# Attention, Fourier mixing and MLP on one core: another PSUM bank for one bound, and landmark sums tied to the planner's clock

## The chip, the core and the metric

The kernel runs on one core of a Trainium2 chip. The time of a run is device microseconds. TensorE (PE) multiplies matrices; VectorE (DVE), ScalarE (ACT) and GpSimd (POOL) work on elements; SyncE (SP) starts the DMAs. Each engine runs its own queue in order, and what one engine writes for another is handed over by semaphores. PE writes into eight PSUM banks of 2 KB in each partition.

## What is computed

The input is q, k and v for 8 batches, 8 heads, 576 tokens and 64 columns a head, and two weights. First comes attention over 32 landmarks a head (each is the mean of 18 tokens):

```python
q_lm = q.reshape(B, H, m, S // m, D).mean(axis=3)
k_lm = k.reshape(B, H, m, S // m, D).mean(axis=3)
A = sm(q, k_lm); Bm = sm(q_lm, k_lm); C = sm(q_lm, k)      # softmaxes
Z = Bm.transpose(0, 1, 3, 2) / (norm1(Bm) * norminf(Bm) + 1e-06)
for _ in range(6):
    Z = 2 * Z - Z @ Bm @ Z
x = A @ Z @ C @ v
```

Then `x` (heads side by side: 576 x 512 a batch) gets the real part of its 2-D Fourier transform added, each token is normalised, and an MLP follows:

```python
u = x + real(fft(fft(x, axis=1), axis=2))
un = (u - mu) / np.sqrt(var + 1e-06)
return u + np.maximum(un @ w_ch1, 0.0) @ w_ch2      # 512 -> 2048 -> 512
```

## The kernel before

Batches are counted from 0, as `b`. The MLP works on chunks of 256 tokens (`TCH` = 2 tiles of 128), of which the 8 batches give 18. Its factors are split into a high and a low half in float16, and each product is three PE products: hi x hi, hi x lo, lo x hi. `h<-unT,w` is its first product, `acc<-w,h` its second; between them ACT and DVE turn a PSUM bank `h` into the tile `h` (ACT the high half, DVE the low one). `unT` is the normalised, transposed tokens of a chunk, `u` the tokens before normalising; `u<-acc` is DVE's last sum, which frees a bank `acc`.

PSUM is divided by hand: four banks are called `at` and serve all of the attention, two are called `h` (`PSH` = 2), two `acc`. A new `at` or `h` tile takes the bank that was used longest ago, and its first product waits until all readers of that bank are done.

The order of PE's instructions is set by a planner at build time. `Kernel.run` holds threads (Python generators), in order of priority: attention (with its helpers `landmarks` and `values`), weights, MLP. A clock `self.now` advances by an estimated cost for each PE instruction. A thread yields how long it wants to be left alone; `till(...)` gives that from the planned end (`self.there`) of the tiles that it needs and from the planned readers of `at` banks, plus a margin. While attention pauses, the MLP's products are put into the queue. In batches 0 and 1 the weights are still being scaled and split (`w<-w,wsc`), and where there is nothing to do yet, PE multiplies a constant (`idle`) so that it doesn't stand.

DVE, ACT and POOL get their order from a scheduler that has its own model of times. The class `Timed` wraps the three: it estimates when each instruction starts, and can tie an instruction behind another of the same engine. The number `late` does that: the instruction is held behind the last one whose planned start is not after `late`.

```python
late = max([late] + [self.kernel.there.get(key(a), 0.0) for a in aps if key(a) in self.kernel.slow and a is not out])
...
prev = next((p for s, p in reversed(self.log) if s <= late), None)
```

`late` is zero unless the code sets it, or the instruction reads something marked as slow (a load, a DMA transpose, a result of POOL). Without such a tie the scheduler may put an instruction wherever its own model finds room.

What happens in one batch, with the names that the profile shows:

- `tokens` starts with the landmark sums `lm`: six DVE reductions over groups of 18 tokens of the loads `big` (per half `e` of the heads: one of k with 1152 elements, two of q with 576 each), and ACT's sums of |q| (`big,amax`). From them come powers of two as scales: `kmax`, `qsum`, `aq_e`, `aq_r` (its reciprocal), `kb`, and by one small product with a matrix of ones (`at<-kb,ones`) and `power` the scale `ak_e`. This is `bound`. Then q and the landmarks are split into halves (`big<-big,aq_r`: ACT writes the high half, DVE the low one; per half of the heads one of 1024 and one of 128 elements).
- `landmarks` computes the logits of the landmarks of q against those of k, and against all of k (`at<-big,lm`, four `at` banks at once). DVE takes `Bd` out of the first two, makes its softmax (`bmx`, `bs`), `nrm` (the softmax and a diagonal of its sums), and `BT`, `BTd`; it takes maxima of all four (`cmx`, `cb`), and ACT writes their exponentials as `mid`. With the banks free again, PE multiplies `nrm` by ones (`at<-nrm,ones_bd`), and six Newton steps follow (`at<-RE,E`).
- `values` transposes the exponentials. From batch 2 on: ACT and POOL split them, two DMA transposes write them back, DVE adds the two halves (`mid<-mid`, 128 x 640), and PE multiplies by v (`at<-big,mid`).
- `mix` multiplies everything together per 128 tokens: `w<-at,scw` is a Fourier term, `u` the sum. `norm` follows: `bn`, `mv`, `ve`, `rt`, `r`, then `row<-u,mv,r`, which ACT casts and POOL or DVE subtracts, and two DMA transposes a tile (`unT<-row`). In batches 0 and 1 the last steps differ a little; up to chunk 1 PE transposes.

The landmark sums of the next batch need only its loads, so DVE may run them early, during the mix of the batch before.

Of the kernel before, what the change touches and what calls it, by code (L numbers as in the profile page):

```python
# [10 lines left out]
F32 = mybir.dt.float32  # L11
# [7 lines left out]
P = 128  # L19
# [16 lines left out]
MARGIN, NM, AM, M0 = 1.5, 2.0, 2.0, 0.2  # L36
# [11 lines left out]
HOLD = 2.5  # L48
# [110 lines left out]
class Kernel:  # L159
# [82 lines left out]
    def mm(self, out, a, b, start=True, stop=True, share=1.0):  # L242
        self.there[out.name] = self.now
        self.now += share * (1.0e-3 if a.dtype == F32 else 0.42e-3) * math.prod(b.shape[1:])
        self.nc.tensor.matmul(out, a, b, start=start, stop=stop, skip_group_check=True)  # L245

    def tr(self, out, a, ident):
        self.there[out.name] = self.now
        self.now += 0.11
        self.nc.tensor.transpose(out, a, ident)  # L250
# [7 lines left out]
        self.A.activation(hi, src, AF.Copy, scale=scale)  # L258
        self.V.scalar_tensor_tensor(lo, src, scale, hi, ALU.mult, ALU.subtract)

    def bound(self, cols, n, factor, name):

        ps = self.psum()
        self.mm(ps[:, :n], self.ones16, cols[:, :n])
        return self.power(ps[:, :n], n, factor, name)

# [155 lines left out]
    def tokens(self, b, st):  # L422

        nc, mm, mm3, tr, sm, split = self.nc, self.mm, self.mm3, self.tr, self.sm, self.split
        V, A = self.V, self.A
# [5 lines left out]
        qhs = []  # L431
        for e in range(2):
            kf, qf = loads[e][0][:, 0 : 2 * S], loads[e][1][:, 0:NQ]
            first = V.tensor_reduce(lm[:, 1, e], kf.rearrange("p (m t) -> p m t", t=18), AX.X, ALU.add)
            if b == 1:
                self.tc.keep_in_program_order(first)

            lv = lm[:, 0, e].rearrange("p (x o m) -> p x o m", o=2, m=8)
            qv = qf.rearrange("p (x o t) -> p x o t", o=2, t=2 * SEG)
            for o in range(2):  # L440
                first = V.tensor_reduce(lv[:, :, o], qv[:, :, o, o : o + 144].rearrange("p x (m t) -> p x m t", t=18), AX.X, ALU.add)
                if b == 1:
                    self.tc.keep_in_program_order(first)
            qhs.append(self.big().bitcast(F16))
            A.activation((self.whole[0].bitcast(F16) if b == 0 else qhs[e])[:, 0:NQ], qf, AF.Abs, accum_out=am[:, e : e + 1])
            yield self.till(lm)
        kb = self.small(2, "kb", BF16)
# [5 lines left out]
        V.tensor_tensor(qs, am[:, 0:1], am[:, 1:2], ALU.add)  # L453
        eq, rq = self.power(qs, 1, 2.0**-13, "aq", b == 1)
        V.tensor_tensor(kb[:, 0:1], km, eq, ALU.mult)
        yield self.till(kb, banks=1, more=AM) + (HOLD if b == 1 else 0.0)
        ek, rk = self.bound(kb, 1, 2.0**-13, "ak")
        sc = self.small(2, "sc")
        V.tensor_tensor(sc[:, 0:1], eq, rk, ALU.mult)
        V.tensor_scalar(sc[:, 1:2], ek, 1.0 / 144.0, None, ALU.mult)  # L460
# [19 lines left out]
        for u in range(3):  # L480
            yield self.till(*qhs, banks=1)
            ps = self.psum()
# [27 lines left out]
        for u in range(3):  # L510
            ae, w = aes[u], 512 if u < 2 else 128
            AT = (self.mid() if u < 2 else self.row()).bitcast(F16)[:, 0 : 2 * w].rearrange("p (y t) -> p y t", y=2)
            if b < 2:
                yield self.till(ae, banks=1)
                ps = self.psum()
# [3 lines left out]
            if b >= 2 or u == 2:  # L519
                yield self.till(ae)  # L520
                hl = self.row(2 * w, F16).rearrange("p (y t) -> p y t", y=2)
# [43 lines left out]
    def values(self, b, st, loads, Ces, crs, ci):  # L565

        nc, mm, tr, sm = self.nc, self.mm, self.tr, self.sm
        V, A = self.V, self.A
        R0 = sm.tile([P, 2, 64], F32, name="R0", bufs=1)
        ETs = []  # L570
        for g in range(2):
            yield self.till(Ces[g])
            if b < 2:
                ET = self.mid().rearrange("p (t m) -> p t m", t=5)
                ps = self.psum()
                for t in range(4):
                    tr(ps[:, 128 * t : 128 * t + 128], Ces[g][:, 128 * t : 128 * t + 128], self.ident)
                A.copy(ET[:, 0:4].rearrange("p t m -> p (t m)"), ps)
                ps = self.psum()
                tr(ps[:64, 0:128], Ces[g][:, 512:576], self.ident)  # L580
                A.copy(ET[:64, 4], ps[:64, 0:128])
            else:

                hl, th = (self.mid().bitcast(F16).rearrange("p (y t) -> p y t", y=2) for _ in range(2))
                A.copy(hl[:, 0], Ces[g])
                self.G.tensor_tensor(hl[:, 1], Ces[g], hl[:, 0], ALU.subtract)
                for y in range(2):
                    nc.sync.dma_start_transpose(th[:, y].rearrange("p (t m) -> p t m", m=P), hl[:, y])
                self.there[th.name] = self.there[hl.name] + 4.0
                self.slow.add(th.name)  # L590
                V.tensor_tensor(Ces[g], th[:, 0], th[:, 1], ALU.add)
                ET = Ces[g].rearrange("p (t m) -> p t m", t=5)
            ETs.append(ET)
        for g in range(2):
            yield self.till(ETs[g], loads[0][2], loads[1][2], banks=1)
            vfs = [loads[e][2].rearrange("p (c d) -> p c d", c=5) for e in range(2)]
            ps = self.psum()
            for t in range(5):
                n = P if t < 4 else 64
                for i in range(4):  # L600
                    e, at = divmod(sum(GROUPS, []).index(HEADS[g][i]), 4)
                    v = vfs[e][:n, t, 64 * at : 64 * at + 64]
                    mm(ps[32 * i : 32 * i + 32, 0:64], ETs[g][:n, t, 32 * i : 32 * i + 32], v if at % 2 == i % 2 else v[:, ::-1], t == 0, t == 4)
            V.tensor_scalar(R0[:, g], ps[:, 0:64], crs[g], ci[:, g : g + 1], ALU.mult, ALU.mult)
        st["R0"] = R0
# [480 lines left out]
```

## Time and profile before

| | |
|---|---|
| runs (three) | 1008.21, 1006.84, 1006.77 us; median 1006.84 |
| profiled execution | 1008.58 us, of which the span is 1006.8 |
| PE, matmuls | 959.8 us busy, 95% of the span, 8698 instructions |
| DVE | 600.5 us, 60% |
| ACT | 333.0 us, 33% |
| POOL | 102.8 us, 10% |
| DMA | 74.66 MB moved, mean 74 GB/s |
| costliest PE groups | first product 411.4 us, second product 386.2 us |
| all landmark sums on DVE | 48, 44.4 us |

A row of the timeline has the start in us, the busy time, the engine, the code line, the operation, the output and inputs by name with the shape, and a count where equal instructions follow each other; in brackets stands how long the engine stood before it, and what it waited for. All lines are 245 (products) or 138 (DVE, ACT and POOL, through `Timed`), so one goes by the names. A row of the windows has the stretch, its sum and mean length, and then for PE, the weight loads, DVE, ACT and POOL the busy time with the number of instructions, then the granted clock of PE and the DMA share.

### The profile page before, as it was taken

What the parts mean: (1) busy time and instruction counts of PE and PEld (TensorE: products, weight loads), DVE (VectorE), ACT (ScalarE), POOL (GpSimd) and SP (SyncE); (2) the same over time, 40 slices, a digit from 0 to 9 for tenths busy, and PEclk for the clock granted to TensorE, in tenths of its full rate; (3) what the DMA queues carried; (4) which work ended last, traced back from release to release, by engine and by line L of the source; (5) the groups of instructions that cost most, each with busy time, mean ns of one, the idle gap of its engine ahead of it and who ended that gap; (6) DMA issues with size and microseconds to landing.
All of it is one profiled execution on the core that took longest, in us unless ns stands there. A gap on an engine that the chain in (4) does not pass through costs nothing.

```text
span 1006.8 us, 20849 instructions
## 1 busy us (share of the span) xinstructions
PE 959.8 (95%) x8698; PEld 666.9 (66%) x8698; DVE 600.5 (60%) x1629; ACT 333.0 (33%) x716; POOL 102.8 (10%) x114
## 2 busy tenths in 40 slices
PE   6869989699999999999999999999999999999998
PEld 4658556467766767667666677676666776666665
DVE  7989876878476836388367736684643935241111
ACT  5668543243224322143224222332322323111110
POOL 0000000003011301032012201120020210010000
PEclk8879989989999999999999999999999999999999
DMA  9854104123302340134211340225020200120000
GB/s 330 290 210 145 62 2 169 22 54 83 136 17 48 63 157 12 32 51 100 100 43 29 45 168 9 55 44 187 1 53 22 53 10 22 22 54 21 1 21 21
DMA packets 97774, 74.66 MB, mean 74 GB/s; under 512 B 68112, under 2 KB 86544, under 8 KB 97552
## 3 DMA queue, kind: packets, MB, share of 16 engines
q1 hardware_dynamic: 97680, 73.34, 25.4%
q8 instruction: 68, 1.11, 0.4%
q14 instruction: 26, 0.21, 0.1%
HBM read 48.02 MB, written 9.44 MB: 57 GB/s over the span
## 4 chain that ended last, share of the span: by engine, by line
PE 86%; DVE 9%; ACT 2%; DMA 2%; issue 1%; POOL 1%; SPq 0%; DVEq 0%; ACTq 0%; POOLq 0%
PE acc L245 36%; PE h L245 36%; PE at L245 13%; DVE w L138 2%; DVE mid L138 1%; DVE u L138 1%; DVE lm L138 1%; DMA big<-k_dram 1%; PE at L250 1%; DVE row L138 0%; ACT w L138 0%; DMA mid<-mid 0%; DMA out_dram<-u 0%; DVE asum L138 0%; DVE bn L138 0%
## 5 line engine op out<-in xcount | busy, mean ns | idle before, releaser
L245 PE MATMUL h<-unT,w 128*128 128x256 f16 x3456 | 411.4, 273 | 6.7 <-DMA unT<-row 5.4
L245 PEld LDWEIGHTS <-w 128*128 128x128 f16 (+1 forms) x3584 | 346.0, 99 | 80.9 <-DMA unT<-row 5.8
L245 PE MATMUL acc<-w,h 128*128 128x512 f16 x1632 | 386.2, 382 | 1.8 <-DVE w L138 1.8
L245 PEld LDWEIGHTS <-h 128*128 128x128 f16 x1632 | 157.8, 99 | 166.6 <-issue 14.2
L138 DVE SCALAR_TENSOR_TENSOR h<-h 128x512 f16<-128x512 f32 x136 | 93.6, 688 | 207.1 <-ACT h L138 206.7
L138 ACT ACTIVATE h<-h 128x512 f16<-128x512 f32 x136 | 81.0, 596 | 319.2 <-PE h L245 313.1
L138 POOL TENSOR_TENSOR r<-ve,mhalf 128x2 f32<-128x2 f32 (+1 forms) x20 | 13.8, 689 | 495.7 <-DVE ve L138 477.0
L138 DVE TENSOR_REDUCE lm<-big 128x32 f32<-128x576 f32 (+1 forms) x48 | 44.4, 938 | 3.3 <-DMA big<-k_dram 3.1
L245 PEld LDWEIGHTS <-big 128*128 128x128 f16 (+1 forms) x864 | 40.5, 104 | 8.5 <-issue 2.1
L138 DVE TENSOR_TENSOR mid<-mid 128x256 f32<-128x256 f32 (+3 forms) x64 | 38.4, 633 | 7.9 <-DMA mid<-mid 6.4
L138 POOL TENSOR_TENSOR mid<-mid 128x640 f16<-128x640 f32 (+1 forms) x24 | 30.6, 1292 | 117.0 <-ACT mid L138 102.5
L245 PEld LDWEIGHTS <-mid 64*128 64x128 f16 (+1 forms) x624 | 29.2, 95 | 17.1 <-issue 10.8
L138 POOL TENSOR_TENSOR row<-row 128x512 f16<-128x512 f32 (+1 forms) x33 | 34.1, 1048 | 50.1 <-ACT row L138 50.1
L138 DVE SCALAR_TENSOR_TENSOR u<-at,scw,w 128x128 f32<-128x128 f32 (+3 forms) x105 | 33.7, 388 | 7.2 <-PE at L245 5.5
L138 ACT CAST row<-row 128x512 f16<-128x512 f32 (+1 forms) x40 | 20.8, 551 | 51.6 <-DVE row L138 44.6
L138 DVE SCALAR_TENSOR_TENSOR w<-at,scw,w 128x262 f32<-128x262 f32 (+1 forms) x42 | 19.1, 486 | 29.7 <-ACT w L138 29.6
L138 DVE SCALAR_TENSOR_TENSOR u<-acc,wsc,u 128x512 f32<-128x512 f32 x36 | 26.9, 749 | 11.8 <-PE acc L245 11.7
L245 PE MATMUL at<-mid,big 128*128 128x262 f16 (+1 forms) x288 | 33.2, 289 | 0.0
L245 PEld LDWEIGHTS at<-RE,E 128*128 128x128 f32 x192 | 26.8, 194 | 8.4 <-issue 2.8
L245 PE MATMUL at<-RE,E 128*128 128x64 f32 (+1 forms) x192 | 28.8, 273 | 3.2 <-DVE E L138 2.5
L138 DVE SCALAR_TENSOR_TENSOR big<-big,aq_r 128x1024 f16<-128x1024 f32 (+1 forms) x32 | 25.8, 840 | 3.5 <-ACT big L138 3.5
L138 DVE TENSOR_TENSOR E<-at,mask 128x256 f32<-128x256 f32 x40 | 16.7, 418 | 18.3 <-PE at L245 18.3
(178 smaller groups left out, 916.8 us busy)
## 6 DMA issues: line engine op xcount, KB each, us to landing
w<-w_dram SPq DMA_DIRECT2D x22, 512.0 KB, 7.0
big<-v_dram SPq DMA_DIRECT2D x16, 640.0 KB, 9.5
big<-q_dram SPq DMA_DIRECT2D x16, 584.0 KB, 6.1
big<-k_dram SPq DMA_DIRECT2D x16, 576.0 KB, 5.2
out_dram<-u SPq DMA_DIRECT2D x36, 256.0 KB, 2.0
big<-w_dram SPq DMA_DIRECT2D x10, 512.0 KB, 6.6
t<-t_dram SPq DMA_DIRECT2D x1, 1048.0 KB, 10.6
unT<-row SPq DMA_TRANSPOSE x64, 2.4
```

The lines of the kernel that those rows point to most:

```text
L138: ins = call(out, *args, **kw)
L245: self.nc.tensor.matmul(out, a, b, start=start, stop=stop, skip_group_check=True)
L250: self.nc.tensor.transpose(out, a, ident)
```

## The change

Three edits. In `bound`, batch 1 takes a bank `h` for the product with ones, instead of an `at` bank; the planner then doesn't wait for an `at` bank there. In `tokens`, each reduction `lm` gets `V.late` set to the planner's clock at that point, and the sum of |q| after it gets `A.late`; so each stands behind every instruction of its engine that the planner has starting before that moment. In `values`, the planned time from the split exponentials to their transposes goes from 4.0 to 6.5, and DVE's add and PE's product with v are planned from it.

```diff
-    def bound(self, cols, n, factor, name):
+    def bound(self, cols, n, factor, name, apart=False):
 
-        ps = self.psum()
+        ps = self.ps_h.tile([P, 512], F32, name="h") if apart else self.psum()
         self.mm(ps[:, :n], self.ones16, cols[:, :n])
...
             kf, qf = loads[e][0][:, 0 : 2 * S], loads[e][1][:, 0:NQ]
+            V.late = A.late = self.now
             first = V.tensor_reduce(lm[:, 1, e], kf.rearrange("p (m t) -> p m t", t=18), AX.X, ALU.add)
...
             for o in range(2):
+                V.late = self.now
                 first = V.tensor_reduce(lv[:, :, o], qv[:, :, o, o : o + 144].rearrange("p x (m t) -> p x m t", t=18), AX.X, ALU.add)
...
-        yield self.till(kb, banks=1, more=AM) + (HOLD if b == 1 else 0.0)
-        ek, rk = self.bound(kb, 1, 2.0**-13, "ak")
+        yield self.till(kb, banks=b != 1, more=AM) + (HOLD if b == 1 else 0.0)
+        ek, rk = self.bound(kb, 1, 2.0**-13, "ak", b == 1)
...
                     nc.sync.dma_start_transpose(th[:, y].rearrange("p (t m) -> p t m", m=P), hl[:, y])
-                self.there[th.name] = self.there[hl.name] + 4.0
+                self.there[th.name] = self.there[hl.name] + 6.5
```

What stands where now. Three places matter below. The first is batch 1's bound. On PE, the difference is one row (`ones_102` is the matrix of ones):

```order
 L245 MATMUL at<-big,lm 32x288 x16
 L245 LDWEIGHTS ones_102
-L245 MATMUL at<-kb,ones_102 128x1
+L245 MATMUL h<-kb,ones_102 128x1
 L245 LDWEIGHTS h
 L245 MATMUL acc_1680<-w_74,h 128x512
```

The product stands at the same place in the queue and only its bank is another. PE's order stays the same up to batch 2's `values`. On ACT, at the beginning of the same stage (`w_74<-w_74,wsc` are splits of the second weight):

```order
 L138 ACTIVATE w_74<-w_74,wsc 128x512 x3
 L138 ACTIVATE unT<-h 128x512
-L138 ACTIVATE w_74<-w_74,wsc 128x512 x2
-L138 ACTIVATE big,amax<-big 128x1168
-L138 ACTIVATE w_74<-w_74,wsc 128x512 x4
+L138 ACTIVATE w_74<-w_74,wsc 128x512 x5
+L138 ACTIVATE big,amax<-big 128x1168
+L138 ACTIVATE w_74<-w_74,wsc 128x512
 L138 ACTIVATE big,amax<-big 128x1168
```

The first of the two sums of |q| has moved behind three splits.

The second place is DVE during batch 1's mix, where the landmark sums `lm` are those of batch 2. Before:

```order
L138 SCALAR_TENSOR_TENSOR w_74<-at,scw,w_73 128x262 x2
L138 TENSOR_REDUCE lm<-big 128x64
L138 SCALAR_TENSOR_TENSOR u<-at,scw,w_74 128x256
L138 SCALAR_TENSOR_TENSOR u<-at,scw,w_74 128x128 x2
L138 SCALAR_TENSOR_TENSOR u<-at,scw,w_74 128x256
L138 SCALAR_TENSOR_TENSOR u<-at,scw,w_74 128x128 x2
L138 BN_STATS bn<-u 128x6 x2
L138 BN_AGGR mv<-bn 128x2
L138 TENSOR_REDUCE lm<-big 128x4x8
L138 BN_AGGR mv<-bn 128x2
L138 SCALAR_TENSOR_TENSOR h<-h 128x512
L138 TENSOR_SCALAR ve<-mv 128x2
```

With the change:

```order
L138 SCALAR_TENSOR_TENSOR w_74<-at,scw,w_73 128x262 x2
L138 SCALAR_TENSOR_TENSOR u<-at,scw,w_74 128x256
L138 SCALAR_TENSOR_TENSOR u<-at,scw,w_74 128x128 x2
L138 SCALAR_TENSOR_TENSOR u<-at,scw,w_74 128x256
L138 SCALAR_TENSOR_TENSOR u<-at,scw,w_74 128x128 x2
L138 BN_STATS bn<-u 128x6 x2
L138 BN_AGGR mv<-bn 128x2 x2
L138 TENSOR_SCALAR ve<-mv 128x2
L138 SCALAR_TENSOR_TENSOR h<-h 128x512
L138 TENSOR_TENSOR rt<-r_2574 128x2
L138 SCALAR_TENSOR_TENSOR rt<-rt,ve 128x2
L138 SCALAR_TENSOR_TENSOR r_2576<-rt,r_2574 128x2
```

Of the four sums that stood between `w` and `row`, two are among the rows before and two came right behind `ve`; all four have left. `ve`, `rt`, `r` and, next in the queue, `row` follow upon `u` with nothing but one `h` between.

The third place is DVE's queue at batch 4's landmarks, behind the last normalising of batch 3. From its `row` to `Bd`, before:

```order
L138 TENSOR_SCALAR row<-u,mv,r_5698 128x512
L138 SCALAR_TENSOR_TENSOR big<-big,aq_r 128x1024
L138 SCALAR_TENSOR_TENSOR big<-big,aq_r 128x128
L138 SCALAR_TENSOR_TENSOR big<-big,aq_r 128x1024
L138 SCALAR_TENSOR_TENSOR h<-h 128x512
L138 SCALAR_TENSOR_TENSOR big<-big,aq_r 128x128
L138 SCALAR_TENSOR_TENSOR h<-h 128x512
L138 TENSOR_SCALAR Bd<-at 128x32 x2
```

With the change, from behind that `row`:

```order
L138 SCALAR_TENSOR_TENSOR h<-h 128x512
L138 TENSOR_REDUCE lm<-big 128x64
L138 TENSOR_REDUCE lm<-big 128x4x8 x2
L138 TENSOR_REDUCE kmax<-lm 128x1
L138 TENSOR_TENSOR qsum<-amax 128x1
L138 TENSOR_SCALAR aq_e<-qsum 128x1
L138 TENSOR_SCALAR aq_e<-aq_e 128x1
L138 RECIPROCAL aq_r<-aq_e 128x1
L138 TENSOR_TENSOR kb<-kmax,aq_e 128x1
L138 SCALAR_TENSOR_TENSOR big<-big,aq_r 128x1024
L138 SCALAR_TENSOR_TENSOR h<-h 128x512
L138 TENSOR_SCALAR Bd<-at 128x32 x2
```

Three of the six sums, and the small steps on them, now stand between `row` and the splits; two of the four splits have moved behind `Bd`. From the last `cb<-cmx` to `BTd`, before:

```order
L138 TENSOR_REDUCE cb<-cmx 128x1
L138 RECIPROCAL bs<-bs 128x2
L138 TENSOR_SCALAR cb<-cb 128x1
L138 TENSOR_TENSOR nrm<-Bd,bs 128x2x32
L138 TENSOR_REDUCE rs<-nrm 128x2
L138 STREAM_TRANSPOSE BT<-nrm 128x32 x2
L138 TENSOR_TENSOR nrm<-diag,rs 128x2x32
L138 TENSOR_TENSOR BTd<-BT,mask 128x256
```

And with the change:

```order
L138 TENSOR_REDUCE cb<-cmx 128x1
L138 RECIPROCAL bs<-bs 128x2
L138 SCALAR_TENSOR_TENSOR big<-big,aq_r 128x128
L138 TENSOR_TENSOR nrm<-Bd,bs 128x2x32
L138 TENSOR_SCALAR cb<-cb 128x1
L138 SCALAR_TENSOR_TENSOR big<-big,aq_r 128x1024
L138 TENSOR_REDUCE rs<-nrm 128x2
L138 STREAM_TRANSPOSE BT<-nrm 128x32 x2
L138 TENSOR_TENSOR nrm<-diag,rs 128x2x32
L138 TENSOR_TENSOR BTd<-BT,mask 128x256
```

The splits stand on both sides of the first `nrm` now. On PE, from batch 2 on, the products with v (`at<-big,mid`) and the first ones behind them stand later among the MLP's products than before.

## The prediction

> **What bounds the kernel now.** Batches count from 0, as `b` in the code. I read the busy shares first, then PE's timeline for every idle time, the chain of waits, and the DVE and ACT queues round each of them.
>
> ```profile
> PE 959.8 (95%) x8698; PEld 666.9 (66%) x8698; DVE 600.5 (60%) x1629; ACT 333.0 (33%) x716; POOL 102.8 (10%) x114
> 100.00:200.00 100.00, 85.42 (x813) 56.34 (x810) 76.98 (x209) 42.28 (x91) 3.75 (x5) 0.95 0.20 65
> 800.00:900.00 100.00, 100.00 (x834) 69.35 (x831) 45.09 (x120) 22.85 (x52) 14.56 (x13) 1.00 0.12 30
> ```
>
> PE is the bound: 959.8 of 1006.8 us, and full from 800 on. Its instructions stay the same ones, so the change is worth what PE's waits lose and gain. They sit in two places. The first is batch 1, between 120 and 210:
>
> ```profile
> 126.04 2.54 PE L245 MATMUL acc<-w,h 128*128 128x512 f16 x11 [1.84 <-DVE w L138]
> 133.75 0.16 PE L245 MATMUL at<-kb,ones 128*128 128x1 bf16 x1 [3.99 <-ACT mid L138]
> 133.78 6.48 PE L245 MATMUL acc<-w,h 128*128 128x512 f16 x18
> 140.10 0.38 PE L245 MATMUL at<-nrm,ones_bd 128*128 128x128 f32 x2
> 149.76 2.75 PE L245 MATMUL acc<-w,h 128*128 128x512 f16 x12
> 194.92 0.49 PE L245 MATMUL at<-Wx,mid 64*128 64x128 f16 x11 [2.37 <-DVE w L138]
> 198.59 0.40 PE L245 MATMUL h<-unT,w 128*128 128x256 f16 x1 [3.18 <-DMA unT<-row]
> 201.18 3.81 PE L245 MATMUL h<-unT,w 128*128 128x256 f16 x17 [2.19 <-DMA unT<-row]
> ```
>
> The bound of k stands 3.99 us for a logits bank that ACT's exponentials (`mid`) free. Afterwards the clock is low: 18 products take 6.48 us there, where 12 take 2.75 later (18 would be 4.1), so 2.4 us more are lost.
>
> The second place is the later batches, where PE has little left to win but stands close behind DVE's landmark chain:
>
> ```profile
> 320.98 1.23 PE L245 MATMUL at<-big,lm 64*32 64x288 f32 x16 [0.79 <-DVE u L138]
> 448.67 0.38 PE L245 MATMUL at<-nrm,ones_bd 128*128 128x128 f32 x2
> 560.87 0.63 PE L245 MATMUL at<-RE,E 128*128 128x64 f32 x4 [2.46 <-DVE E L138]
> 561.93 4.45 PE L245 MATMUL acc<-w,h 128*128 128x512 f16 x12
> 660.33 0.39 PE L245 MATMUL at<-nrm,ones_bd 128*128 128x128 f32 x2
> 780.69 1.23 PE L245 MATMUL at<-big,lm 64*32 64x288 f32 x16 [0.80 <-DVE u L138]
> ```
>
> **Part 1: the bound takes an `h` bank (batch 1).** No instruction is added or removed.
>
> ```profile
> 115.14 1.16 ACT L138 ACTIVATE big<-big 128x1168 f16<-128x1168 f32 x1
> 128.61 1.16 PE L245 MATMUL at<-big,lm 64*32 64x288 f32 x29
> 128.89 0.15 DVE L138 TENSOR_TENSOR kb<-kmax,aq_e 128x1 bf16<-128x1 f32 x1
> 134.87 0.18 DVE L138 TENSOR_TENSOR nrm<-diag,rs 128x64 f32<-128x64 f32 x1
> ```
>
> `kb` is there at 129.0, and PE ends the logits at 129.8, so in the new bank the bound runs at once: the 3.99 go, and with them the low clock. But the 18 products after it then end 3.9 us later, at 133.7, and the next in PE's queue reads `nrm`, which DVE writes at 135.05: a new wait of 1.3. The same stage gains at its head: ACT's sum of |q| (1.16) now stands behind three more splits of w, so DVE's splits, and all behind them to `nrm`, come 1.1 earlier, which takes 1.1 of the 1.84. PE's product with `nrm` thus moves from 140.1 to about 134.0: 135.05 - 1.1, and I take **-6.0**. Ends: -4.9 if the head gains nothing, -7.4 if `nrm` is no wait. The `h` bank is free (its last product ended at 112), and `ak_e` reads it long before the next `h` needs it: nothing.
>
> **Part 2: the landmark sums stand behind the mix.** The queue of DVE in batch 1's mix, before:
>
> ```profile
> 184.66 1.34 DVE L138 TENSOR_REDUCE lm<-big 128x64 f32<-128x1152 f32 x1
> 189.01 0.72 DVE L138 TENSOR_REDUCE lm<-big 128x32 f32<-128x576 f32 x1
> 193.47 0.99 DVE L138 TENSOR_SCALAR row<-u,mv,r 128x512 f32<-128x512 f32 x2
> 194.69 5.23 SPq L907 DMA_TRANSPOSE unT<-row  x4
> 426.88 1.27 DVE L138 BATCH_NORM_STATS2 bn<-u 128x6 f32<-128x512 f32 x2
> 429.96 1.00 DVE L138 TENSOR_SCALAR row<-u,mv,r 128x512 f32<-128x512 f32 x2
> ```
>
> In a queue a row costs its length less 0.08: 1.26 and 0.64. Four sums stand ahead of `row`, whose cast starts the four transposes for which PE waits. Without them: `u` starts at 185.0, when PE's Wx products are there, and ends at 186.9; batch 3's rows show 3.08 from bn to `row` without sums: 190.0. That is 3.5 before 193.47. The transposes shift alike, so **-3.5** at 201.18; the wait at 194.92 lies inside that. Ends: -1 (something else late) and -4. The clock stays low there, since PE still stands 4.6 of 5 us.
>
> The six sums (5.1 us) are not gone. They now stand behind the mix, shortly ahead of PE's logits. Batch 4, before:
>
> ```profile
> 310.91 0.16 DVE L138 RECIPROCAL aq_r<-aq_e 128x1 f32<-128x1 f32 x1
> 312.31 1.28 DVE L138 SCALAR_TENSOR_TENSOR big<-big,aq_r 128x1024 f16<-128x1024 f32 x1 [1.17 <-ACT big L138]
> 437.27 0.55 DVE L138 TENSOR_SCALAR row<-u,mv,r 128x512 f32<-128x512 f32 x1
> 443.10 0.29 DVE L138 TENSOR_SCALAR Bd<-at 128x32 f32<-128x32 f32 x2
> 446.26 0.18 DVE L138 TENSOR_TENSOR nrm<-diag,rs 128x64 f32<-128x64 f32 x1
> ```
>
> Walked with these lengths from 429.96: two sums (1.9) before `w`, one (0.64) and an `h` (0.6) before and behind bn, and the third `row` starts at 438.2 instead of 437.27. Then `row` 0.47, `h` 0.6, three sums 2.54, `kmax` 0.2, four small steps 0.55: `aq_r` starts at 442.56. ACT's half of the first q split needs it, and DVE's follows 1.4 behind `aq_r` (310.91 to 312.31): 443.96. That split 1.2, `h` 0.6: `Bd` at 445.8 instead of 443.10. From `Bd` to the end of `nrm` it was 3.3; now a split of 0.26 and one of 1.20 stand between: 450.5. PE wants it at 448.67: **+1.9**.
>
> The same walk elsewhere, in before's time:
>
> ```profile
> 226.02 0.38 PE L245 MATMUL at<-nrm,ones_bd 128*128 128x128 f32 x2
> 305.80 0.69 DVE L138 SCALAR_TENSOR_TENSOR h<-h 128x512 f16<-128x512 f32 x1 [1.29 <-ACT h L138]
> 309.06 0.88 DVE L138 SCALAR_TENSOR_TENSOR w<-at,scw,w 64x262 f32<-64x262 f32 x2 [2.57 <-ACT w L138]
> 321.37 0.27 DVE L138 TENSOR_SCALAR Bd<-at 128x32 f32<-128x32 f32 x2
> 545.95 0.28 DVE L138 TENSOR_SCALAR Bd<-at 128x32 f32<-128x32 f32 x2
> 551.05 0.39 PE L245 MATMUL at<-nrm,ones_bd 128*128 128x128 f32 x2
> 559.57 0.82 DVE L138 TENSOR_TENSOR mid<-mid 128x640 f32<-128x640 f16 x1 [2.23 <-DMA mid<-mid]
> 654.76 0.29 DVE L138 TENSOR_SCALAR Bd<-at 128x32 f32<-128x32 f32 x2 [1.39 <-PE at L245]
> ```
>
> - Batch 3: three sums behind the `h` at 305.80 (to 308.95), the `w` of 309.06 as before to 309.9, the next `h` at 311.55, three sums, `kmax`, small steps: `aq_r` at 315.5, the split 316.9 to 318.0, `h`, two `u<-acc` at 0.67, splits 0.26 and 1.20, `Bd` and a maximum 0.57: 322.0. Only then come the `u` (0.92) that free the last two logits banks; they ended at 321.37. The second half of the logits runs from 323.0 instead of 320.98: **+2.0**. Batch 7 has the same order and the same 0.80: **+2.0**.
> - Batch 6: `Bd` at 658.1 instead of 654.76, then 3.3 and a split of 0.26: 661.7 against PE's 660.33: **+1.4**.
> - Batch 5: `Bd` at 547.6 instead of 545.95; `nrm` at 550.9 is just in time for 551.05, but the exponentials, their transposes, DVE's add and `E` behind it come 1.6 later (the add of 559.57 starts as its transposes land), and PE waits for that `E` already: **+1.6**.
> - Batch 2: `u<-acc` is 0.8 late for PE's first product of a new chunk, `nrm` (226.02) another 0.8: **+1.6**.
>
> Ends for these six (10.5 in all): 3, if only the two bank waits and half of the rest reach PE; 14, if the queue is 0.6 slower at each.
>
> **Part 3: 4.0 to 6.5.** It puts PE's products with the transposed tile later, among first products that fill PE: nothing. It does not pull `E` out from behind the add in batch 5, where the order still has add, then `E`; so the 2.46 stay.
>
> **The clock.** A wait of 1.84 at 126.04 left 11 products at 2.54, full speed; one of 2.46 at 560.87 made 12 take 4.45 instead of 2.75: 1.7 lost. My waits in batches 3 and 7 are 2.8 each. Between the two ends, 0 and 1.7, I take 1.0 each, nearer the row with the nearest wait: **+2.0**. [...]
>
> **The sum:** -6.0 - 3.5 + 1.9 + 2.0 + 2.0 + 1.4 + 1.6 + 1.6 + 2.0 = **+3.0 us**. The profiled execution took 1008.6 (span 1006.8), 1.7 over the median of the runs, 1006.84; so the profile goes to about 1011.6 and the median to about **1009.8**.
>
> **Rivals.** What a measurement of this kernel can tell from no change is about 0.2%, 2 us.
> - *DVE catches up in time (faster).* DVE is only 60% busy, and its queue waits for ACT and PE at many places in these stages. If `nrm` in batches 2, 4 and 6 still meets PE, the price there is nil and only the bank waits of 3 and 7 and batch 5's `E` remain: -9.5 + 2 x 1.5 + 1.0 = -5.5: 1001.3. It decides at `nrm`: 0.2 us or less of wait. Against it: 448.67 leaves 2.3 us behind before's 446.4, and 5.1 us of sums and 1.5 of splits go in.
> - *The terms cancel (within 0.2%).* The walk as above, but the waits of 3 and 7 straddle whatever the clock looks at: +1.0: 1007.8.
> - *Every late wait cools PE (much slower).* If 1.9 in batch 4 is enough too and `E` falls behind the adds in batches 4 and 6: the 2.0 for the clock become 5.1 and 1.5 is added: +7.6: 1014.4. The 1.84 that cost no clock speaks against it.
> - *The bound gains nothing,* because PE meets `nrm` at once where it met the bank: then -6.0 is -1.1 and the sum +7.9: 1014.7. The rows give `nrm` only 1.3 us of it.
>
> **Chances.** The forecast 0.40, both slow rivals together 0.15, cancelling 0.27, catching up 0.18. So slower 0.55, same 0.27, faster 0.18. Forecast alone: 1008.9 to 1012. The range for 8 in 10 cuts the outer half of the fast case and of the slow ones: 1002.5 to 1014.5.
>
> **What would show it.** In the changed profile: no wait at the `h<-kb` product, one of about 1.3 at `nrm` behind it; `at<-nrm` near 134 and first `unT` products near 191.5; idle time ahead of `at<-nrm` in batches 2, 4, 6 (1 to 2 us each), ahead of the second half of the logits in 3 and 7 (near 2.8, "DVE u"), and about 4 at batch 5's `RE,E`. If those at `nrm` are missing, the walk is wrong and the kernel is faster; if the stage up to 205 gains less than 8, it is slower than I say.

## The result, and the profile after

The changed kernel takes 1017.37 us (median of 4 runs, 1016.06 to 1018.86) against 1007.4 of the kernel before (1006.77 to 1008.21): ratio 1.0099, interval 1.0081 to 1.0116. It is 10 us slower; forecast were 3. The profiled execution has a span of 1016.9 against 1006.8, so the two traces carry the whole difference. PE is busy 4.3 us longer than before (959.8) with the same number of products, and stands 5.8 longer. Its row:

```profile
PE 964.1 (95%) x8698; PEld 668.4 (66%) x8698; DVE 602.0 (59%) x1629; ACT 331.8 (33%) x716; POOL 100.5 (10%) x114
```

Batch 1 in PE's timeline after the change:

```profile
125.61 2.53 PE L245 MATMUL acc<-w,h 128*128 128x512 f16 x11 [1.50 <-DVE w L138]
129.27 0.18 PE L245 MATMUL h<-kb,ones 128*128 128x1 bf16 x1
129.31 4.04 PE L245 MATMUL acc<-w,h 128*128 128x512 f16 x18
134.83 0.46 PE L245 MATMUL at<-nrm,ones_bd 128*128 128x128 f32 x2 [1.48 <-ACT mid L138]
188.51 0.49 PE L245 MATMUL at<-Wx,mid 64*128 64x128 f16 x11 [0.90 <-DVE w L138]
190.24 0.40 PE L245 MATMUL h<-unT,w 128*128 128x256 f16 x1 [1.24 <-DMA unT<-row]
192.85 3.81 PE L245 MATMUL h<-unT,w 128*128 128x256 f16 x17 [2.21 <-DMA unT<-row]
```

The 3.99 at the bound are gone, the 18 products behind it run at full speed (4.04 in place of 6.48, with a granted clock of 1.00 in place of 0.61), and `nrm` is a wait of 1.48. The transposes come 8.3 us sooner than before (192.85 against 201.18). So batch 1 does what it should. The waits in the later batches, in the same view:

```profile
210.60 1.46 PE L245 MATMUL acc<-w,h 128*128 128x512 f16 x6 [1.52 <-DVE u L138]
219.23 0.46 PE L245 MATMUL at<-nrm,ones_bd 128*128 128x128 f32 x2 [0.35 <-DVE nrm L138]
316.29 1.72 PE L245 MATMUL at<-big,lm 64*32 64x288 f32 x16 [2.55 <-DVE u L138]
445.79 0.16 PE L245 MATMUL at<-kb,ones 128*128 128x1 bf16 x1 [1.65 <-ACT mid L138]
549.96 0.16 PE L245 MATMUL at<-kb,ones 128*128 128x1 bf16 x1 [0.91 <-ACT mid L138]
561.33 0.63 PE L245 MATMUL at<-RE,E 128*128 128x64 f32 x4 [2.67 <-DVE E L138]
661.77 0.16 PE L245 MATMUL at<-kb,ones 128*128 128x1 bf16 x1 [2.09 <-ACT mid L138]
686.73 0.66 PE L245 MATMUL at<-RE,E 128*128 128x64 f32 x4 [1.90 <-DVE RE L138]
687.23 4.45 PE L245 MATMUL h<-unT,w 128*128 128x256 f16 x24
789.08 1.23 PE L245 MATMUL at<-big,lm 64*32 64x288 f32 x16 [2.56 <-DVE u L138]
```

Of these only 316.29, 561.33 and 789.08 had a wait before, and two of the three were 0.8. To see what each batch costs, take one row that stands at the same place of every batch, the first logits of the landmarks. Two of them, before and then after:

```profile
653.89 0.27 PE L245 MATMUL at<-lm 64*32 64x32 f32 x13
779.11 0.27 PE L245 MATMUL at<-lm 64*32 64x32 f32 x13
```

```profile
654.39 0.27 PE L245 MATMUL at<-lm 64*32 64x32 f32 x13
785.74 0.27 PE L245 MATMUL at<-lm 64*32 64x32 f32 x13
```

Between them lies batch 6: 0.50 behind at its start, 6.63 at its end, so 6.1 lost. The same with the other batches (batch 1 starts with the products ahead of its first wait, 123.17 before and 123.08 after, and ends with the second product behind its mix, 207.77 and 198.50; the end of batch 7 is that of the span):

| batch | forecast us | measured us |
|---|---|---|
| 1, bound and mix | -9.5 | -9.2 |
| 2 | +1.6 | +2.8 |
| 3 | +2.0, and 1.0 of clock | +3.1 |
| 4 | +1.9 | +2.5 |
| 5 | +1.6 | +1.3 |
| 6 | +1.4 | +6.1 |
| 7 | +2.0, and 1.0 of clock | +3.5 |

With 0.1 that the profiled run was ahead at the start of batch 1, these make the 10.1 of the spans, but for rounding. The forecast counts no clock in batch 6; the low stretch there is in the 6.1.

### The profile page after: what moved, and what is told of

Its sections match the earlier page's. It is cut to its first block, busy times and chain, and to the rows that moved or that the text cites. A ratio compares the mean times of both kernels' runs of the same rounds, so it can differ in the third digit from the quotient of the medians.

```text
span 1016.9 us, 20858 instructions
## 1 busy us (share of the span) xinstructions
PE 964.1 (95%) x8698; PEld 668.4 (66%) x8698; DVE 602.0 (59%) x1629; ACT 331.8 (33%) x716; POOL 100.5 (10%) x114
## 4 chain that ended last, share of the span: by engine, by line
PE 72%; DVE 15%; issue 6%; ACT 3%; DMA 2%; POOL 2%; SPq 0%; DVEq 0%; POOLq 0%; ACTq 0%
PE h L245 30%; PE acc L245 29%; PE at L245 12%; DVE w L138 3%; DVE lm L138 2%; DVE u L138 2%; DVE mid L138 2%; DVE big L138 1%; DVE row L138 1%; DVE h L138 1%; POOL row L138 1%; DMA mid<-mid 1%; ACT big L138 1%; DVE cmx L138 1%; DMA big<-k_dram 1%
## 5 line engine op out<-in xcount | busy, mean ns | idle before, releaser
L138 ACT ACTIVATE big<-big,aq_r 128x1024 f16<-128x1024 f32 (+1 forms) x32 | 23.0, 773 | 17.5 <-DVE kb L138 15.7
```

Of the source, the lines that this page charges most:

```text
L138: ins = call(out, *args, **kw)
```

## The experiments

Theory 1: DVE's late sums make each of batches 2 to 7 pay for itself, the bank only gains, and 6.5 does nothing. Theory 2: the 6.5, which moves PE's products with v, makes the loss. The order of PE's instructions is the same in all kernels with 4.0, and the same in all with 6.5, but for the name of a bank; so these comparisons are clean on PE. Each ratio is against the kernel before, with its 95% interval.

### One part alone

The bank alone:

```diff
+        ps = self.ps_h.tile([P, 512], F32, name="h") if apart else self.psum()
+        yield self.till(kb, banks=b != 1, more=AM) + (HOLD if b == 1 else 0.0)
+        ek, rk = self.bound(kb, 1, 2.0**-13, "ak", b == 1)
```

> The bound's new bank alone (landmark sums free, 4.0 as before). PE's order is that of before but for the name of one bank. Theory 1 (the sums' places cost, the bank only gains): the 3.99 us wait and the low clock behind it go, a wait at nrm of about 2.4 us comes, since DVE's chain is not earlier here: -4.9 us against before, nothing from batch 2 on. Theory 2 (the planner's 6.5 costs): the same here. If the gain at the head of that stage in the changed kernel came from the bank, -6.

Measured: 1003.26 us, ratio 0.9944 (0.9929 to 0.9959). From batch 2 on it has the waits of before and no other. The wait at `nrm`, in PE's timeline and in DVE's:

```profile
133.96 0.46 PE L245 MATMUL at<-nrm,ones_bd 128*128 128x128 f32 x2 [1.48 <-ACT mid L138]
```

```profile
133.63 0.18 DVE L138 TENSOR_TENSOR nrm<-diag,rs 128x64 f32<-128x64 f32 x1
```

The product starts 0.15 behind the end of DVE's write of `nrm` (133.81), so it is `nrm` for which PE waits, though the row names ACT.

The late sums alone:

```diff
+            V.late = A.late = self.now
             first = V.tensor_reduce(lm[:, 1, e], ...)
...
+                V.late = self.now
                 first = V.tensor_reduce(lv[:, :, o], ...)
```

> The late landmark sums alone (bound in an at bank, 4.0). PE's order is that of before. Theory 1: batch 1's mix gains 4.8 us and the head of the bound's stage about 1, and batches 2 to 7 lose what they lose in the changed kernel, 21: about +15 us against before, with the waits for ACT's mid at the bound of k in batches 4, 5 and 6 (1.7, 0.9, 2.1) and the wait at the Newton steps of batch 6. Theory 2 (the 6.5, by later products with v and so later R and E, makes the loss at batch 6's Newton steps and part of the others): only about +9, and no low clock in batch 6.

Measured: 1024.15 us, ratio 1.0148 (1.0131 to 1.0164), +15.6. The waits that theory 1 named at the bound of k are there (1.66, 0.90 and 2.10 in batches 4 to 6), and those at the logits' second half. The bank of batch 1 still has its wait:

```profile
135.47 0.16 PE L245 MATMUL at<-kb,ones 128*128 128x1 bf16 x1 [3.99 <-ACT mid L138]
324.62 1.72 PE L245 MATMUL at<-big,lm 64*32 64x288 f32 x16 [2.56 <-DVE u L138]
670.92 0.16 PE L245 MATMUL at<-kb,ones 128*128 128x1 bf16 x1 [2.10 <-ACT mid L138]
```

The wait at batch 6's Newton step is not there as named: 0.48 in place of 1.90, with two waits ahead of it (0.55 and 1.26), which the kernel with 4.0 below has too. Batch 6 has no low clock in this trace, as theory 2 had said; but the time is that of theory 1.

The 6.5 alone:

```diff
-                self.there[th.name] = self.there[hl.name] + 4.0
+                self.there[th.name] = self.there[hl.name] + 6.5
```

> The planner's 6.5 alone. Theory 1: within 1 us of before, batch 5's wait for E (2.46) as before. Theory 2: +4 us or more, with a wait at a Newton step of batch 6 behind R.

Measured: 1008.85 us, ratio 1.0002 (0.9991 to 1.0014). Nothing.

The changed kernel with 4.0 (the last diff undone):

> The changed kernel with 4.0 instead of 6.5 (bank and late sums). Theory 1: as the changed kernel, +10 us against before, with 3 to 4 us lost at batch 6's Newton steps. Theory 2: +4 to +6, no wait at batch 6's Newton steps.

Measured: 1018.73 us, ratio 1.0095 (1.0078 to 1.0112), as the changed kernel. The loss at batch 6 is there (5.95 between the two rows of logits), but at another place: PE stands at the products with v, in two waits (0.84 and 1.26), and the clock goes low: the 9 second products right behind take 3.05, the next 9 take 2.11. PE's rows and DVE's:

```profile
676.01 0.90 PE L245 MATMUL at<-big,mid 128*32 128x64 f32 x40 [0.84 <-issue]
678.17 1.45 PE L245 MATMUL at<-big,mid 128*32 128x64 f32 x40 [1.26 <-DVE asum L138]
```

```profile
673.16 0.83 DVE L138 TENSOR_TENSOR mid<-mid 128x640 f32<-128x640 f16 x1 [3.52 <-DMA mid<-mid]
675.22 0.69 DVE L138 TENSOR_TENSOR mid<-at,amx 128x512 f32<-128x512 f32 x1
677.35 0.68 DVE L138 TENSOR_TENSOR mid<-at,amx 128x512 f32<-128x512 f32 x1
```

The added tile is there at 673.99, long before. Each half of the products starts 0.10 and 0.14 behind the end of a `mid<-at,amx` (675.91, 678.03), a step of the tokens' softmax that reads an `at` bank. So, read from these times, PE waits for `at` banks that DVE frees late, since the softmax stands behind the late add in its queue.

So the three parts are worth -5.3, +15.6 and +0.3 by these medians, together +10.6 where the change as a whole gave +10. Theory 2 has fallen: the 6.5 only moves the place in batch 6 where PE stands.

### DVE or ACT, and each batch by itself

The changed kernel without `A.late`:

```diff
-            V.late = A.late = self.now
+            V.late = self.now
```

> The changed kernel without A.late: ACT's sums of |q| go back to their places of before, DVE's sums stay late. Theory 1 (DVE's queue is the price): within 2 us of the changed kernel, the same waits at the bound of k in batches 4 to 6 and at the second half of the logits in 3 and 7. Rival (the sums of |q| come too late for aq_e, and DVE only waits for them): most of the loss goes, 1011 or less, and those waits with it.

Measured: 1012.98 us, ratio 1.0052 (1.0031 to 1.0073): between the two expectations, so theory 1 as I had put it, within 2 us of the changed kernel, missed. The waits in batches 3, 5, 6 and 7 are there (2.28, 0.98, 1.47, 2.24); in batch 4 PE stands 1.32 for `lm` instead. Most of the difference lies in batch 6, which costs 1.7 here. By the medians DVE's late sums, with the bank's gain, thus make +5.7, and the late sums of |q| 4 more, in good part by what happens in batch 6 (below), and that is not ACT's work alone.

Late sums up to batch 2 only, with the bank and 4.0:

```diff
-            V.late = A.late = self.now
+            if b <= 2:
+                V.late = A.late = self.now
...
-                V.late = self.now
+                if b <= 2:
+                    V.late = self.now
```

> Bank, and late sums in batches 0 to 2 only; 4.0. Theory 1 (each batch pays for its own late sums): batch 1 gains 4.9 for the bank and 3.4 in the mix, a low clock there is one window shorter (0.9), batch 2 loses about 3, and from batch 3 on the distance to the kernel before stays: -6 in all, 1 better than the bank alone. Rival (a delay once made returns at every batch, or the loss hangs on where PE's waits fall against the clock, so that it comes in the later batches all the same): +2 or more, with waits in batches 3 to 7 that the kernel before doesn't have.

Measured: 1004.99 us, ratio 0.9965 (0.9951 to 0.998). Batches 3 to 7 have the waits of the kernel before (0.78, 2.59 at `E`, 0.81) and lose nothing: the rival has fallen. But it is -2.3 and not -6 by the medians of 12 runs. In its profiled execution the part behind 118 us is 6.0 faster than in that of the kernel before, as expected, and the part ahead of it, in which the orders are the same up to 115 us, 2.2 slower. One profile doesn't say what the middle run has, so what the late sums of batch 2 are worth on balance stays open; the bank alone was faster.

Late sums in batch 6 alone (bank, 6.5), with ACT's and then without:

```diff
-            V.late = A.late = self.now
+            if b == 6:
+                V.late = A.late = self.now
...
-                V.late = self.now
+                if b == 6:
+                    V.late = self.now
```

> Bank, 6.5, and late sums (DVE's lm and ACT's sums of |q|) in batch 6 alone. Theory 1 (each batch pays for its own late sums): up to batch 5 as the bank alone (-5 against before), then batch 6 loses what it lost in the changed kernel, 6 to 7 (2.1 at the bound of k, 1.9 at a Newton step behind DVE's second add, 1.7 of low clock): +1.5 against before, and nothing in batch 7. Rival (batch 6's second part came from the batches before it): a loss of 2 to 3 only, -2.5 against before.

> As the kernel with late sums in batch 6 alone, but ACT's sums of |q| are left where they were before; only DVE's sums are late. If the late sums of |q| carry batch 6's second part (the casts of mid then stand elsewhere in ACT's queue), batch 6 loses 2 to 3 here: -2.5 against before. If DVE's sums carry all of it, it loses 6 to 7 as with both: +1.5.

Measured: 1007.54 us (0.9996, 0.9982 to 1.0011) and 1005.54 us (0.9973, 0.9958 to 0.9988), by the medians -0.7 and -2.7; the first is 2 better than expected. Between the rows of logits batch 6 costs 6.1 and 3.6; batch 7 costs nothing. So batch 6's price is its own. Without ACT's part the wait at the bound is 0.6 shorter, the wait at the Newton step stays (1.50 in place of 1.81), and the low clock behind it is missing (the first 13 products there take 1.58 us; with ACT's part 24 take 4.38). My expectation for the second, 2 to 3 in batch 6, was a little short, since the Newton step's wait is there without ACT's late sums too. In the changed kernel without `A.late` it is not there. These two traces differ in how long the transposes of the second tile take (the last section).

### The bank in every batch

```diff
-        yield self.till(kb, banks=b != 1, more=AM) + (HOLD if b == 1 else 0.0)
-        ek, rk = self.bound(kb, 1, 2.0**-13, "ak", b == 1)
+        yield self.till(kb, banks=b < 1, more=AM) + (HOLD if b == 1 else 0.0)
+        ek, rk = self.bound(kb, 1, 2.0**-13, "ak", b > 0)
```

> The changed kernel with the bank of the first product for the bound of k in every batch from 1 on (0 keeps at). The orders of all engines are the same; only the bank's name differs. Theory 1 (DVE's chain is the price, whatever stands in front of it): the waits at the bound of k in batches 4, 5 and 6 (1.65, 0.91, 2.09) go, and PE stands as long at nrm in batches 4 and 6 and at E in batch 5: within 1 us of the changed kernel. Rival (the bank is the price there, as it was in batch 1): 4 us faster, 1013.

Measured: 1020.05 us, ratio 1.0107 (1.0087 to 1.0126). No gain; the interval overlaps with that of the changed kernel. PE's waits have moved one step down the queue, as theory 1 says:

```profile
447.74 0.46 PE L245 MATMUL at<-nrm,ones_bd 128*128 128x128 f32 x2 [1.98 <-ACT RE L138]
561.57 0.63 PE L245 MATMUL at<-RE,E 128*128 128x64 f32 x4 [3.35 <-DVE E L138]
663.18 0.46 PE L245 MATMUL at<-nrm,ones_bd 128*128 128x128 f32 x2 [1.79 <-DVE nrm L138]
```

1.65 became 1.98, 2.09 became 1.79, and the 0.91 of batch 5 went into the wait for `E` (2.67 to 3.35). A bank helps only where what stands behind it is ready.

### Two versions with fewer late sums

Only the sums of batch 2 are held, and only behind the first `row` of batch 1's mix (bank, 4.0); the second version differs in 20.0 for 16.0:

```diff
-            V.late = A.late = self.now
+            if b == 2:
+                V.late = self.now - (9.0, 16.0)[e]
...
-                V.late = self.now
+                if b == 2:
+                    V.late = self.now - (9.0, 16.0)[e]
```

> Bank; 4.0; sums held only in batch 2, and less: behind the first row of batch 1's mix (planner's clock less 9 and less 16 us for the two halves), three of them ahead of the second row, three behind it. Theory 1: the mix's 3.4 and the 0.9 of clock stay won, and batch 2 loses 1 to 2 in place of 3, since DVE has half of its sums behind it when batch 2's chain begins: -7.5, 1001. If what counts in batch 2 is the last three sums alone, which stand right ahead of the sum u<-acc as in the changed kernel, it is -6, as with late sums to batch 2.

> As the kernel with sums behind the first row, but the second half's sum of k (1.34) stands ahead of that row, between ve and rt, where DVE waits for POOL's power in part, and only two sums stand behind the second row. Theory 1: 0.6 to 1.3 of the mix's 3.4 are lost, and batch 2 loses about 1 in place of 3: -7, 1001.5.

Measured: 1005.22 us (0.998, 0.9967 to 0.9992; runs from 1000.58 to 1007.47) and 1002.03 us (0.9943, 0.9925 to 0.9962). The second and the bank alone (0.9944) are the fastest kernels here, faster than both the kernel before and the changed one, and not told apart. Forecast were -7.5 and -7; by the medians -2.1 and -5.2 came. The first missed clearly: in its profile the span is 998.5, but most of its runs are slower, and its batch 2 still waits 1.35 at the bound and 1.47 at `nrm`. The mix's gain is real in each profile, and is paid back in batch 2 in part in each.

## Why the prediction was wrong, point by point

- **Batch 1's bound: right in kind, -6.0 was too much.** PE's product with `nrm` stands at 134.83, not 134.0. The 1.1 at the head did not come: PE's first wait went from 1.84 to 1.50 only. ACT's queue behind its sums of |q| waits for DVE's `w` (1.60 us with the bank alone, 0.69 with all three parts), so it was DVE and not ACT that set the pace there. That is the end that I gave for this, -4.9: the product row behind, 153.90 before, is at 148.96.
- **The mix: right.** -3.5 were forecast; the transposes' row moved 3.4 more than the bound had (8.3 - 4.9). The low clock there lasts 6.83 us in place of 10.24, worth the rest of the 9.2.
- **Part 3: right**, as the kernel with 6.5 alone shows.
- **The walk through DVE's queue in batches 2 to 7: right in mechanism, too short.** `Bd` of batch 6 was to be at 658.1 in the time of before; it is at 659.15, with PE 0.5 later there: 658.65. Batches 3, 4, 5 and 7 came within 0.6 of the forecast. Batch 2 lost 2.8 and not 1.6: `u<-acc` was 1.5 late and not 0.8. In batches 4 to 6 PE meets the late chain one step ahead of `nrm`, at the bound of k, whose bank ACT's exponentials hold. The walk had not looked there; the price is nearly the same, as the kernel with the bank in every batch shows.
- **Batch 6, +1.4: the step that failed.** The walk stopped at `nrm`. I followed the exponentials further in batch 5 only. In batch 6 they are late as well, and behind them stand the split, the transposes, DVE's add of the second tile, and in DVE's queue 12 us of work (softmax of the tokens, `R`) up to `E` and `RE` of the third Newton step. There PE stands 1.90 more, and the clock goes low (a granted 0.50 from 688.14 to 691.55): 24 products take 4.45 and not 2.78. The two are 3.6 of the 4.7 that were missed here (6.1 - 1.4); another 0.7 is the wait at the bound, 2.09 where 1.4 were forecast. But the late exponentials alone do not make the 3.6: the transposes behind them took 1.8 longer than before, which no walk through DVE's queue could give. In the changed kernel without `A.late`, where they did not, batch 6 cost 1.7, near the forecast.
- **The clock: 1.0 each for batches 3 and 7 was between the ends; the upper end came.** Three new low stretches (batches 3, 6, 7; 3.41 us each at a granted 0.50) cost 1.7 each in this profile. That is chance in part: with 4.0 the same wait in batch 7 was followed by a clock of 1.00 (last section). The rival "every late wait cools PE", at 1014.4, comes nearest in kind: the clock fell behind three of the late waits, but not behind that of batch 4 (1.65); and it alone let `E` wait for the late adds in batch 6. The rival at 1014.7 is nearer by its number alone; its mechanism, that the bound gains nothing, did not happen.

What carries batch 6's second part is seen in DVE's and POOL's rows. After:

```profile
664.49 2.75 POOL L138 TENSOR_TENSOR mid<-mid 128x640 f16<-128x640 f32 x2 [14.63 <-ACT mid L138]
```

```profile
669.08 0.82 DVE L138 TENSOR_TENSOR mid<-mid 128x640 f32<-128x640 f16 x1
673.41 0.83 DVE L138 TENSOR_TENSOR mid<-mid 128x640 f32<-128x640 f16 x1 [3.52 <-DMA mid<-mid]
685.76 0.41 DVE L138 TENSOR_TENSOR E<-at,mask 128x256 f32<-128x256 f32 x1
```

Without `A.late`, in the same place:

```profile
666.01 2.76 POOL L138 TENSOR_TENSOR mid<-mid 128x640 f16<-128x640 f32 x2 [13.51 <-ACT mid L138]
```

```profile
672.93 0.82 DVE L138 TENSOR_TENSOR mid<-mid 128x640 f32<-128x640 f16 x1 [1.03 <-DMA mid<-mid]
685.30 0.40 DVE L138 TENSOR_TENSOR E<-at,mask 128x256 f32<-128x256 f32 x1
```

POOL starts 1.5 later there, and the second add is 0.5 earlier: 6.92 from the one to the other, against 8.92 in the changed kernel. Before it was 7.14. The last section says what the difference of about 2 us is.

How much hangs on it can be estimated from the same rows. DVE ends the `RE` for which PE waits 13.3 behind the start of the second add, in both traces. With the 7.14 of before in place of 8.92 it would be there at 684.9, and PE, whose wait of 1.90 begins at 684.83, would stand about 0.1. The low clock that follows that wait would probably be missing too. By this estimate the 3.6 needs both the late exponentials and the slow transposes. Of the six kernels compared here with late sums in batch 6, five (changed, 4.0, both with late sums in batch 6 alone, bank in every batch) have 8.8 to 9.0 from POOL's start to the second add; only the changed kernel without `A.late` has 6.92, near the 7.14 of before. What makes the five slow, and not that one, stays open.

## What to carry to other kernels

Work that is held back on an engine that is only 60% busy is not free: look at what stands behind its new place, and whether the busiest engine waits for that, once per batch. Follow a late chain to its last reader and not to its first, since in a queue in order the delay is handed on to work that has nothing to do with it. A change of several parts is worth taking apart even when each part is small: here one part gave 5 us and another took 15.

## What the runs showed of the hardware

**What a wait cost in clock went with where it fell.** All of this is measured in this kernel's traces. The clock's records give the low stretches (a granted 0.50). Behind the first 118 us and up to 1000 us they last, in the kernel before, from 131.91 to 138.74, 196.76 to 207.00 and 561.99 to 565.40; in the changed kernel from 189.79 to 196.62, 316.09 to 319.50, 561.85 to 565.26, 688.14 to 691.55 and 790.54 to 793.95. Each is one, two or three times 3.41 us long, and within a trace their starts lie whole multiples of 3.41 apart. Marks 3.41 apart can thus be laid through a trace, so that every one of these stretches starts and ends on a mark; call the stretch between two of them a cell. Two traces have the same wait in batch 7, 2.56 and 2.55 us. In the changed kernel most of it lies in one cell (windows of three cells; after the length stands PE's busy time, and further right, ahead of the last two numbers, the granted clock):

```profile
783.71:787.13 3.42, 2.81 (x45) 1.31 (x43) 3.42 (x6) 1.80 (x4) 0.00 (x0) 1.00 0.09 33
787.13:790.54 3.41, 1.46 (x19) 0.59 (x20) 3.41 (x12) 0.26 (x1) 0.00 (x0) 1.00 0.33 121
790.54:793.95 3.41, 3.41 (x18) 2.45 (x17) 2.89 (x20) 2.04 (x8) 0.00 (x0) 0.50 0.02 5
```

With 4.0 in place of 6.5 it lies across two:

```profile
783.88:787.30 3.42, 2.18 (x42) 1.03 (x40) 3.42 (x6) 1.18 (x2) 0.00 (x0) 1.00 0.27 102
787.30:790.71 3.41, 2.09 (x25) 1.15 (x26) 3.41 (x15) 0.26 (x1) 0.00 (x0) 1.00 0.16 56
790.71:794.12 3.41, 3.41 (x24) 2.02 (x22) 2.85 (x19) 2.96 (x11) 0.00 (x0) 1.00 0.00 0
```

1.95 idle in one cell are followed by a low cell (0.50); 1.24 and 1.32 in two cells are not (1.00). Counted in the same way in the two traces of before and after, from 118 to 1000 us: the eight cells at full clock with 1.69 to 2.92 us of idle time were each followed by a low one, and none of those with 1.65 or less was. That is a count of two traces and gives no limit for others.

Against the kernel's work the marks lie elsewhere in each of the two: the low stretch of batch 5 starts 1.12 us behind PE's product with `E` before (560.87), and 0.52 behind it after (561.33). One kernel's runs come in groups; that the first makes the second is not shown, but fits. Among 22 runs of the kernel before, those with a mean clock of 0.979 to 0.984 took 1006.35 to 1007.42 us, those with 0.976 took 1008.15 to 1009.28, and those with 0.974 or less 1011.40 to 1011.49. A few microseconds can thus not be read from one run.

**A fetch of instructions stood ahead of a DMA's last packets.** The 2 us in batch 6: in the changed kernel the transposes' last packets wait. DMA from 670 to 671.14, in 40 slices, and then to 672.38:

```profile
GB/s 27 45 27 90 126 189 216 234 207 189 207 252 260 207 180 189 278 216 207 198 216 171 207 225 225 171 189 225 234 154 82 612 18 18 0 0 0 0 0 0
q8 instruction: 1, 0.02, 6.8%
```

```profile
GB/s 0 0 0 0 0 0 0 0 0 0 0 0 0 0 0 0 0 0 0 0 0 0 0 0 0 0 0 0 0 0 0 0 8 8 8 8 8 0 0 0
DMA packets 7, 0.00 MB, mean 1 GB/s; under 512 B 7, under 2 KB 7, under 8 KB 7
```

A fetch of 16 KB (queue 8, the 612) begins at 670.91, as the data end, and takes 1.24 us by its record; seven packets of the transposes move only from 672.14 on, and DVE's add starts 1.1 behind the last of them. In the kernel before and in the changed one without `A.late` the fetch comes behind the last packets (667.71 against 667.13, and about 673.1 against 672.3); there the add starts 0.6 behind the last packet, and is 7.14 and 6.92 behind POOL's start, against 8.92 in the changed kernel. That the fetch is the cause is read from this order in three traces; no run moved the fetch alone, and for the four other kernels with 8.8 to 9.0 its place is not shown.
